# Moving the transposes of q, k and the attention output from TensorE to crossbar DMA, with a reordered start

## The chip, the cores and the metric

The kernel runs on one core of a Trainium2 chip. The metric is device time of one execution in microseconds (us). Each number quoted as a result is the median of several executions; most executions of one kernel agree within about 0.3%. All runs quoted here are in the fast state. Ratios are the mean time of one kernel's fast runs over the mean of the other kernel's fast runs of the same rounds, so they are not quite the ratio of the medians quoted beside them. In the profiles PE is TensorE, DVE is VectorE, ACT is ScalarE, POOL is GpSimd and SP is SyncE; SBUF and PSUM are the two on-chip memories that hold the kernel's tiles, with the matmul results in PSUM.

## The reference, cut to what matters

```python
# q, k, v: (8 batches, 8 heads, 576 positions, 64), float32
scores = matmul(q, k^T) / 8 + bias[bucket(|i - j|)]      # T5 relative bias, 32 buckets
x = softmax(scores) @ v                                   # (8, 8, 576, 64)
x = x.transpose(0, 2, 1, 3).reshape(4608, 512)
h = x @ w_in                                              # 512 -> 2048
out = max(0.01 * h, h) @ w_out                            # 2048 -> 512, float32
```

## The kernel before

Two heads form a pair, and there are 32 pairs, four to a batch. For each pair the kernel computes scores transposed (keys on partitions), takes the exponential on ScalarE, multiplies the diagonal band by the exponentiated bias on VectorE, and multiplies with v on TensorE (`av`). The feed-forward part is cut into 288 *pieces* of four 512-wide matmuls, and up to eight pieces are put into each pair as filler for TensorE. A tile of 512 tokens can start only when all the attention output that it reads is finished; whatever was not placed runs in a tail after the last pair.

Three operands have to be turned: q and k of the pair (12 blocks of 96x128) and the attention output (5 blocks of 128x128, the last half empty). All turns go through TensorE into PSUM, and are copied out:

```python
def transpose_q(n):
    qs = prs.pop((n, "q"))
    ps = ps_m_pool.tile([P, 8 * P], BF16, name="ps_tq", tag="m")
    for c in range(NC):                                   # NC = 6
        nc.tensor.transpose(ps[:, c * RQ : (c + 1) * RQ], in_=qs[0:RQ, c, :], identity=ident[0:RQ, 0:RQ])
    ...  # copied to qt by VectorE (ScalarE in pairs 1 to 3)
# transpose_k: the same, into kt
def x_transposes(n):
    ...
    for ic in range(NJ + 1):                              # 5 blocks
        nc.tensor.transpose(ps[:, ic * P : (ic + 1) * P], in_=opair[:, ic, :], identity=ident)
    nc.vector.tensor_copy(out=xT[p][:, b * S : (b + 1) * S], in_=ps[:, 0:S])
```

The order of work inside pair n, shortened (`moe(k)` places up to k pieces, alternating between the first and the second layer):

```python
    pair_rows(n + 1)                     # gathers the pair's q and k rows, VectorE
    scores 0, 1;  moe(1);  av(n - 1, 0);  transpose_q(n + 1);  moe(1)
    scores 2, 3;  moe(1);  av(n - 1, 1);  transpose_k(n + 1);  moe(1)
    scores 4, 5;  moe(1);  x_transposes(n - 1);  finished(n - 1);  moe(1);  moe(2)
moe_rest()                               # after the last pair
```

`finished` releases the token tiles that a batch completes. At the start, the bias rows come from DRAM in the order `hk` for heads 0 and 1, `hk` for heads 2 to 7 (576 KB), `hk4` for the last 64 keys.

The softmax here doesn't subtract the row's maximum and nothing guards it: scores larger than these inputs give would overflow.

Of the kernel before, what the change touches and what calls it, by code (L numbers as in the profile page):

```python
# [11 lines left out]
BF16 = mybir.dt.bfloat16  # L12
# [25 lines left out]
def kernel(  # L38
# [10 lines left out]
    nc = tc.nc  # L49

    B, H, S, D = q.shape
    NB, HH = bias_table.shape
    DM, DF = moe_w_in.shape
    NT = B * S
# [15 lines left out]
    per = ctx.enter_context(tc.tile_pool(name="per", bufs=1))  # L70
    qt_pool = ctx.enter_context(tc.tile_pool(name="qt", bufs=2))
    pr_pool = ctx.enter_context(tc.tile_pool(name="pr", bufs=4))
    op_pool = ctx.enter_context(tc.tile_pool(name="op", bufs=2))
    rc_pool = ctx.enter_context(tc.tile_pool(name="rc", bufs=4))
    gt_pool = ctx.enter_context(tc.tile_pool(name="gt", bufs=2))
# [7 lines left out]
    nc.vector.memset(warm, 0.0)  # L83
    nc.scalar.activation(warm, warm, AF.Exp)

    xT = [per.tile([P, NT], BF16, name=f"xT{p}") for p in range(n_pairs)]
    w_in_sb = per.tile([P, n_cc, DF], BF16, name="w_in_sb")
    w_out_sb = per.tile([P, n_fc, DM], BF16, name="w_out_sb")
    hk = per.tile([P, H, 3 * P], BF16, name="hk")
# [16 lines left out]
    def load_qk(b, h0, h1):  # L106
        i = b % NBUF
        for src, dst in ((q, qn[i]), (k, kn[i])):
            nc.gpsimd.dma_start(
                out=dst[0:RQ, h0:h1, :, :].rearrange("r h c d -> r h (c d)"),  # L110
                in_=src[b, h0:h1, :, :].rearrange("h (r c) d -> r h (c d)", c=NC),
            )

    def load_v(b, h0, h1, by_head):
        i = b % NBUF
        p0, p1 = h0 // 2, h1 // 2
        if by_head:
            for h in range(h0, h1):
                nc.gpsimd.dma_start(
                    out=vn[i][:, :, h, 0:D],  # L120
                    in_=v[b, h, 0 : NJ * P, :].rearrange("(c s) d -> s c d", s=P),
                )
        else:
            for c in range(NJ):
                nc.gpsimd.dma_start(  # L125
                    out=vn[i][:, c, h0:h1, 0:D],
                    in_=v[b, h0:h1, c * P : (c + 1) * P, :].rearrange("h s d -> s h d"),
                )
        for e in range(2):
            nc.gpsimd.dma_start(  # L130
                out=v4[i][e * SL : (e + 1) * SL, p0:p1, e, 0:D],
                in_=v[b, h0 + e : h1 : 2, NJ * P : S, :].rearrange("h s d -> s h d"),
            )

    def clear(eng, i):
        eng.memset(v4[i], 0.0)
        for e in range(2):
            eng.memset(v4[i][e * SL : (e + 1) * SL, :, e, D : D + 1], 1.0)
        eng.memset(vn[i][:, :, :, D : D + 1], 1.0)
        eng.memset(kts_[i][:, S : S + P], 0.0)  # L140
        eng.memset(at_[i][:, ATW : ATW + SL], 1.0)
        eng.memset(at4_[i][:, S : S + SL], 1.0)

    junk = per.tile([P, 512], BF16, name="junk")
    nc.vector.memset(junk, 0.0)
    clear(nc.vector, 0)
    tabT = per.tile([H, NB], FP32, name="tabT")
    with nc.allow_non_contiguous_dma(reason="a table of 256 numbers"):
        nc.sync.dma_start(out=tabT, in_=bias_table.rearrange("u h -> h u"))
# [27 lines left out]
    )  # L177
    udr = nc.dram_tensor("u_row", [H, UW], BF16, kind="Internal")
    nc.sync.dma_start(out=udr.ap(), in_=ub)
    for h0, h1 in ((0, 2), (2, H)):  # L180
        nc.sync.dma_start(
            out=hk[:, h0:h1, :],
            in_=bass.AP(tensor=udr, offset=h0 * UW, ap=[[1, P], [UW, h1 - h0], [1, BW]]),
        )

    for e in range(2):
        nc.sync.dma_start(
            out=hk4[e * SL : (e + 1) * SL, :, :],
            in_=bass.AP(tensor=udr, offset=e * UW + SL + P, ap=[[1, SL], [2 * UW, n_pairs], [1, P + SL]]),
        )  # L190

    def mirrored(t, lo, hi):

# [4 lines left out]
        return bass.AP(tensor=v.tensor, offset=v.offset + hi - lo - 1, ap=ap)  # L198

    load_qk(0, 2, H)  # L200
    load_v(0, 0, 2, True)
    load_v(0, 2, H, False)
    clear(nc.gpsimd, 1)
    load_qk(1, 0, H)

    def load_w_in(half):
# [1 line left out]
        nc.gpsimd.dma_start(out=w_in_sb[:, :, o], in_=moe_w_in[:, o].rearrange("(c p) f -> p c f", p=P))  # L208

    def load_w_out(half):  # L210
        n = n_fc // 2
        nc.gpsimd.dma_start(
            out=w_out_sb[:, half * n : (half + 1) * n, :],
            in_=moe_w_out[half * n * P : (half + 1) * n * P, :].rearrange("(f p) e -> p f e", p=P),
        )


    items = [(b, p) for b in range(B) for p in range(n_pairs)]
    qts, kts, ops_ = {}, {}, {}

    prs = {}

    def pair_rows(n, which):
        src = {"q": qn, "k": kn}[which]
        b, p = items[n]
        t = pr_pool.tile([RQ, NC, 2 * D], BF16, name="pr")
        nc.vector.tensor_copy(out=t.rearrange("r c (e d) -> r c e d", e=2),
                              in_=src[b % NBUF][0:RQ, 2 * p : 2 * p + 2, :, :].rearrange("r e c d -> r c e d"))
        prs[n, which] = t

    def transpose_q(n):
        qs = prs.pop((n, "q"))
        ps = ps_m_pool.tile([P, 8 * P], BF16, name="ps_tq", tag="m")
        for c in range(NC):
            nc.tensor.transpose(ps[:, c * RQ : (c + 1) * RQ], in_=qs[0:RQ, c, :],  # L235
                                identity=ident[0:RQ, 0:RQ])
        qt = qt_pool.tile([P, S], BF16, name="qt")
        o, x = qt.rearrange("p (r c) -> p r c", c=NC), ps[:, 0:S].rearrange("p (c r) -> p r c", c=NC)
        if 0 < n < n_pairs:
            nc.scalar.copy(out=o, in_=x)  # L240
        else:
            nc.vector.tensor_copy(out=o, in_=x)  # L242
        qts[n] = qt

    def transpose_k(n):
        ks = prs.pop((n, "k"))
        ps = ps_m_pool.tile([P, 8 * P], BF16, name="ps_tk", tag="m")
        for c in range(NC):
            nc.tensor.transpose(ps[:, c * RQ : (c + 1) * RQ], in_=ks[0:RQ, c, :],  # L249
                                identity=ident[0:RQ, 0:RQ])  # L250
        kt = kts_[n % 2]
        nc.vector.tensor_copy(out=kt[:, 0:S].rearrange("p (r c) -> p r c", c=NC),  # L252
                              in_=ps[:, 0:S].rearrange("p (c r) -> p r c", c=NC))
        for e in range(2):
            r = slice(e * D, (e + 1) * D)
            nc.vector.tensor_copy(out=kt[r, S + e * SL : S + (e + 1) * SL], in_=kt[r, NJ * P : S])
        kts[n] = kt

    def qk_mm(n, u):

# [55 lines left out]
    def av(n, e):  # L316
# [7 lines left out]
        for ic in range(NJ + 1):  # L324
            for c in range(NJ):
# [7 lines left out]
        nc.vector.tensor_tensor(out=opair[:, :, e * D : (e + 1) * D], in0=ps[:, :, 0:D],  # L333
                                in1=rcp.to_broadcast([P, NJ + 1, D]), op=ALU.mult)

    def x_transposes(n):
        b, p = items[n]
        opair = ops_[n]
        ps = ps_m_pool.tile([P, 8 * P], BF16, name="ps_tx", tag="m")
        for ic in range(NJ + 1):  # L340
            nc.tensor.transpose(ps[:, ic * P : (ic + 1) * P], in_=opair[:, ic, :], identity=ident)  # L341
        nc.vector.tensor_copy(out=xT[p][:, b * S : (b + 1) * S], in_=ps[:, 0:S])
# [52 lines left out]
    def moe(n_pieces):  # L395
        nonlocal turn
        for _ in range(n_pieces):
            piece(("in", "out")[turn], False)
            turn ^= 1
# [5 lines left out]
    def finished(n):  # L405
        b, p = items[n]
        if p == n_pairs - 1:
            while made["ready"] < n_tt and (made["ready"] + 1) * TT <= (b + 1) * S:
                made["ready"] += 1


    pw = ps_o_pool.tile([P, 512], FP32, name="ps_w", tag="ps_o")
    for _ in range(14):
        nc.tensor.matmul(pw, lhsT=junk[:, 0:P], rhs=junk, start=True, stop=True)

    pair_rows(0, "q")
    pair_rows(0, "k")
    transpose_q(0)
    transpose_k(0)
    N = len(items)  # L420
    for n in range(N + 1):
        live = n < N
        if live:
            b, p = items[n]
            if n == 0:
                load_w_in(0)
                load_v(1, 0, H, False)
                load_w_in(1)
                load_w_out(0)
                load_w_out(1)  # L430
            elif p == 1 and 0 < b < B - 1:
                load_qk(b + 1, 0, H)
                load_v(b + 1, 0, H, False)
            if n + 1 < N:
                pair_rows(n + 1, "q")
                pair_rows(n + 1, "k")
            ps_a, ps_b = qk_mm(n, 0), qk_mm(n, 1)
            exp_band(n, 0, ps_a)
        moe(1)
        if live:  # L440
            exp_band(n, 1, ps_b)
        if n > 0:
            av(n - 1, 0)
        if n + 1 < N:
            transpose_q(n + 1)
        moe(1)
        if live:
            ps_a, ps_b = qk_mm(n, 2), qk_mm(n, 3)
            exp_band(n, 2, ps_a)
        moe(1)  # L450
        if live:
            exp_band(n, 3, ps_b)
        if n > 0:
            av(n - 1, 1)
        if n + 1 < N:
            transpose_k(n + 1)
        moe(1)
        if live:
            ps_a, ps_b = qk_mm(n, 4), qk_mm(n, 5)
            exp_band(n, 4, ps_a)  # L460
        moe(1)
        if n > 0:
            x_transposes(n - 1)
            finished(n - 1)
        moe(1)
        if live:
            exp_band(n, 5, ps_b)
        moe(2)
# [31 lines left out]
```

## Time and profile before

| | before |
|---|---|
| median time | 417.23 us (416.54 to 417.75, 3 runs) |
| span in the profile | 414.7 us |
| one pair in the steady part | 11.08 us |
| one pair without filler (pairs 2 to 4) | about 6 us |

The windows view of the kernel before gives, for a stretch of time, the busy time of each engine with the number of instructions, in the order PE, PE weight loads, VectorE, ScalarE, GpSimd, and then the granted TensorE clock as a share of full speed, the DMA share and GB/s. These rows are the starting phase, two moments of it, and the steady part:

```profile
0.00:27.00 27.00, 20.16 (x178) 10.50 (x179) 15.60 (x62) 14.43 (x19) 19.90 (x37) 0.75 1.24 172
16.00:18.00 2.00, 1.48 (x19) 1.05 (x18) 1.14 (x3) 0.94 (x2) 2.00 (x3) 0.50 1.69 193
18.00:20.00 2.00, 0.22 (x5) 0.23 (x6) 0.54 (x3) 0.00 (x0) 1.15 (x2) 0.50 1.42 195
110.00:330.00 220.00, 220.00 (x2316) 113.35 (x2314) 134.24 (x334) 147.37 (x199) 23.95 (x30) 1.00 0.35 52
```

The first busy number is PE. From 110 to 330 us TensorE is busy for all of the 220 us, while VectorE (134.24) and ScalarE (147.37) have slack. (The DMA share exceeds 1 in some rows, so it is used here only to compare.) At 18 to 20 us TensorE does almost nothing, and its clock is at half.

What a transpose costs has to be read from starts, not from the duration of one matmul, because matmuls overlap. The timeline of the kernel before, on TensorE (start, length, engine, line, what it does, how many merged), for the six q, six k and five output transposes, each followed by the next work, and the same matmul in two successive pairs:

```profile
226.27 0.42 PE L235 MATMUL ps_tq<-ident,pr 96*128 96x96 bf16 x6
226.53 1.03 PE L364 MATMUL pm_3608<-w_out_sb,gt 128*128 128x512 bf16 x4
...
229.66 0.42 PE L249 MATMUL ps_tk<-ident,pr 96*128 96x96 bf16 x6
229.92 1.03 PE L364 MATMUL pm_3608<-w_out_sb,gt 128*128 128x512 bf16 x4
...
231.10 0.39 PE L275 MATMUL ps_s<-qt,kt_107 128*128 128x512 bf16 x1
...
232.22 0.44 PE L341 MATMUL ps_tx<-ident,opair 128*128 128x128 bf16 x5
232.50 1.03 PE L364 MATMUL pm_3608<-w_out_sb,gt 128*128 128x512 bf16 x4
...
242.18 0.39 PE L275 MATMUL ps_s<-qt,kt_108 128*128 128x512 bf16 x1
```

The q transposes hold TensorE from 226.27 to 226.53 us, 0.26 us; k likewise 0.26 us; the output 0.28 us. That is 0.80 us of an 11.08 us pair. The Trainium skill's page "VectorE: DVE Perf Modes", section The three transpose paths, gives 390 ns for a 128x128 transpose on TensorE; here the trace shows a mean of 219 ns for one, and five of them take 0.28 us together because they are pipelined.

The waits view of the kernel before (who waited for whom: total us, times, longest) has one line that belongs to the start:

```profile
DVE at_0_111 L314 <- DMA hk_98<-u_row: 2.3, 1, 2.3
```

VectorE waits 2.3 us for `hk4` in pair 0, and TensorE waits behind it. This is the hole at 18 to 20 us.

### The profile page before, as it was taken

What the parts mean: (1) busy time and instruction counts of PE and PEld (TensorE: products, weight loads), DVE (VectorE), ACT (ScalarE), POOL (GpSimd) and SP (SyncE); (2) the same over time, 40 slices, a digit from 0 to 9 for tenths busy, and PEclk for the clock granted to TensorE, in tenths of its full rate; (3) what the DMA queues carried; (4) which work ended last, traced back from release to release, by engine and by line L of the source; (5) the groups of instructions that cost most, each with busy time, mean ns of one, the idle gap of its engine ahead of it and who ended that gap; (6) DMA issues with size and microseconds to landing.
All of it is one profiled execution on the core that took longest, in us unless ns stands there. A gap on an engine that the chain in (4) does not pass through costs nothing.

```text
span 414.7 us, 9081 instructions
## 1 busy us (share of the span) xinstructions
PE 397.0 (96%) x3886; PEld 204.0 (49%) x3886; DVE 222.7 (54%) x573; ACT 248.2 (60%) x342; POOL 59.8 (14%) x87
## 2 busy tenths in 40 slices
PE   7688899999999999999999999999999999999995
PEld 3355455554555555555445554555555454444442
DVE  5489776666666566655665566666556430101011
ACT  2688688766666766666666666667676633333310
POOL 8732410410040102210041004000000000000000
PEclk9589999999999999999999999999999999999999
DMA  8999993917063801872093509100000001010112
GB/s 116 204 197 196 206 163 54 60 32 135 27 42 44 141 26 34 78 115 52 27 82 61 107 28 81 30 19 9 25 27 27 28 27 51 25 53 25 51 51 77
DMA packets 60513, 29.37 MB, mean 71 GB/s; under 512 B 39472, under 2 KB 54840, under 8 KB 60472
## 3 DMA queue, kind: packets, MB, share of 16 engines
q0 software_dynamic: 53408, 18.35, 41.4%
q1 hardware_dynamic: 7064, 10.43, 7.2%
q8 instruction: 30, 0.49, 0.5%
q14 instruction: 11, 0.09, 0.1%
HBM read 37.68 MB, written 9.45 MB: 114 GB/s over the span
## 4 chain that ended last, share of the span: by engine, by line
PE 83%; DVE 7%; ACT 4%; DMA 3%; issue 1%; SPq 0%; DVEq 0%; ACTq 0%
PE ps_o L327 8%; PE ps_s L266 7%; PE ps_s L275 2%; DMA hk_98<-u_row 2%; PE ps_o L329 2%; PE ps_tx L341 2%; PE ps_tq L235 1%; ACT at_109 L286 1%; ACT at_110 L286 1%; PE ps_tk L249 1%; DVE at_109 L314 1%; PE ps_s L272 1%; DMA u_row<-ub 1%; DVE opair L333 1%; ACT gt L355 1%
## 5 line engine op out<-in xcount | busy, mean ns | idle before, releaser
L353 PEld LDWEIGHTS <-w_in_sb 128*128 128x128 bf16 x576 | 49.9, 98 | 72.6 <-issue 21.7
L364 PEld LDWEIGHTS <-gt 128*128 128x128 bf16 x576 | 52.5, 98 | 51.4 <-issue 0.4
L286 ACT ACTIVATE at_109<-ps_s 128x1024 bf16<-128x1024 f32 x64 | 64.5, 1023 | 20.5 <-PE ps_s L266 20.4
L286 ACT ACTIVATE at_110<-ps_s 128x1024 bf16<-128x1024 f32 x64 | 64.7, 1021 | 15.7 <-PE ps_s L266 15.7
L314 DVE TENSOR_TENSOR at_110<-at_110,hk 128x512 bf16<-128x512 bf16 (+1 forms) x64 | 32.2, 506 | 44.5 <-ACT at_110 L286 40.6
L314 DVE TENSOR_TENSOR at_109<-at_109,hk 128x512 bf16<-128x512 bf16 (+1 forms) x64 | 32.0, 506 | 38.6 <-ACT at_109 L286 36.4
L327 PEld LDWEIGHTS <-at_109 128*128 128x128 bf16 x640 | 28.5, 99 | 10.3 <-DVE opair L333 3.0
L333 DVE TENSOR_TENSOR opair<-ps_o,rcp 128x320 bf16<-128x320 f32 x64 | 31.5, 492 | 2.2
L327 PEld LDWEIGHTS <-at_110 128*128 128x128 bf16 x640 | 27.2, 98 | 9.6 <-DVE opair L333 3.0
L125 POOL DMA_DIRECT2D vn_104<-in_v_dram x16 | 14.1, 892 | 72.2 <-PE ps_o L329 71.2
L266 PE MATMUL ps_s<-qt,kt_107 64*128 64x512 bf16 x128 | 20.9, 388 | 2.8 <-DVE kt_107 L252 1.5
L125 POOL DMA_DIRECT2D vn_103<-in_v_dram x16 | 14.0, 887 | 61.7 <-PE ps_o L329 60.0
L242 DVE COPY qt<-ps_tq 128x576 bf16<-128x576 bf16 x29 | 21.7, 748 | 1.8 <-PE ps_tq L235 1.8
L266 PE MATMUL ps_s<-qt,kt_108 64*128 64x512 bf16 x128 | 20.9, 396 | 0.9 <-ACT at_110 L286 0.5
L332 DVE RECIPROCAL rcp<-ps_o 128x5 f32<-128x5 f32 x64 | 12.2, 191 | 11.6 <-PE ps_o L329 11.6
L327 PE MATMUL ps_o<-vn_103,at_109 128*128 128x65 bf16 x320 | 16.3, 200 | 1.1 <-DVE opair L333 0.7
L329 PEld LDWEIGHTS <-at_0_111 128*128 128x128 bf16 x160 | 15.9, 99 | 2.5 <-DVE at_0_111 L314 2.5
L327 PE MATMUL ps_o<-vn_103,at_110 128*128 128x65 bf16 x320 | 14.5, 194 | 1.7 <-DVE opair L333 1.7
L329 PE MATMUL ps_o<-v_0_105,at_0_111 128*128 128x65 bf16 x80 | 13.8, 200 | 2.2 <-DVE at_0_111 L314 2.2
L329 PEld LDWEIGHTS <-at_1_112 128*128 128x128 bf16 x160 | 15.6, 97 | 0.2 <-DVE at_1_112 L314 0.2
L341 PEld LDWEIGHTS <-opair 128*128 128x128 bf16 x160 | 11.3, 98 | 7.6 <-DVE opair L333 0.9
L288 ACT ACTIVATE at_110<-ps_s 128x512 bf16<-128x512 f32 x16 | 9.6, 598 | 9.1 <-PE ps_s L272 9.1
(873 smaller groups left out, 815.2 us busy)
## 6 DMA issues: line engine op xcount, KB each, us to landing
out_dram<-y SPq DMA_DIRECT2D x36, 256.0 KB, 2.0
qn_100<-in_q_dram POOLq DMA_DIRECT2D x4, 576.0 KB, 6.6
kn_102<-in_k_dram POOLq DMA_DIRECT2D x4, 576.0 KB, 9.6
w_in_sb<-in_moe_w_in_dram POOLq DMA_DIRECT2D x2, 1024.0 KB, 13.5
vn_104<-in_v_dram POOLq DMA_DIRECT2D x16, 128.0 KB, 4.8
w_out_sb<-in_moe_w_out_dram POOLq DMA_DIRECT2D x2, 1024.0 KB, 16.9
qn_99<-in_q_dram POOLq DMA_DIRECT2D x3, 576.0 KB, 7.0
kn_101<-in_k_dram POOLq DMA_DIRECT2D x3, 576.0 KB, 9.3
```

The costliest lines, as they stand in the source:

```text
L125: nc.gpsimd.dma_start(out=vn[i][:, c, h0:h1, 0:D], in_=v[b, h0:h1, c * P : (c + 1) * P, :].rearrange("h s d -> s h d"),)
L242: nc.vector.tensor_copy(out=o, in_=x)
L266: nc.tensor.matmul(ps[:, e, :], lhsT=kt[r, u * P : (u + 1) * P], rhs=qt[r, 0:512], start=True, stop=True)
L286: nc.scalar.activation(at[:, :, u, 0:512], ps, AF.Exp, scale=scale)
L314: nc.vector.tensor_tensor(out=o, in0=o, in1=m, op=ALU.mult)
L327: nc.tensor.matmul(ps[:, ic, :], lhsT=at[:, o : o + P], rhs=vn[i][:, c, 2 * p + e, :], start=(c == 0), stop=False)
L329: nc.tensor.matmul(ps[:, ic, :], lhsT=at4[:, ic * P : (ic + 1) * P], rhs=v4[i][:, p, e, :], start=False, stop=True)
L332: nc.vector.reciprocal(rcp, ps[:, :, D : D + 1])
L333: nc.vector.tensor_tensor(out=opair[:, :, e * D : (e + 1) * D], in0=ps[:, :, 0:D], in1=rcp.to_broadcast([P, NJ + 1, D]), op=ALU.mult)
L341: nc.tensor.transpose(ps[:, ic * P : (ic + 1) * P], in_=opair[:, ic, :], identity=ident)
L353: nc.tensor.matmul(pm, lhsT=w_in_sb[:, c, f * P : (f + 1) * P], rhs=xT[c][:, t0 : t0 + TT], start=(c == 0), stop=(c == n_cc - 1))
L364: nc.tensor.matmul(pm, lhsT=gt[:, f, ts * P : (ts + 1) * P], rhs=w_out_sb[:, f, :], start=(f == 0), stop=(f == n_fc - 1))
```

## The change: intent and diff

The intent is to take the transposes off TensorE. A DMA transpose through the crossbar turns the blocks while copying them from SBUF to SBUF. To keep out of the way of the first loads, q and k go by DMA only from pair 10 and the output from pair 6. The rest of the change prepares the start: bias rows for the last keys come before those of heads 2 to 7, a few memsets move from GpSimd to VectorE, w_out is loaded in batch 1, the loads of later batches are spread over the pairs, and "spin" matmuls on zeros keep TensorE busy in pair 0 (at the very start there were 14 of them before and are 15 now). The core of the diff:

```diff
+    load_hk(0, 2)
     for e in range(2): ... hk4 ...
+    load_hk(2, H)
...
+    AHEAD = 3
+    def by_dma(n):
+        return n >= 2 * n_pairs + 2
+    def turn_by_dma(n):
+        t = turned[n] = tu_pool.tile([P, 2 * NC, RQ], BF16, name="tu")
+        nc.sync.dma_start_transpose(out=t, in_=prs.pop(n).rearrange("r j c d -> r (j c d)"))
+    def turned_pair(n, j):
+        if by_dma(n):
+            return turned[n][:, j * NC : (j + 1) * NC, :].rearrange("p c r -> p r c")
+        ...  # six TensorE transposes as before
...
+    def x_by_dma(n):
+        return n_pairs + 2 <= n < N - 1
     def x_transposes(n):
+        if x_by_dma(n):
+            nc.sync.dma_start_transpose(
+                out=xT[p][:, b * S : b * S + w].rearrange("p (i t) -> p i t", t=P),
+                in_=opair.rearrange("p i d -> p (i d)"))
+            return
...
+            elif 0 < b < B - 1:          # loads spread over the pairs of a batch
+                if p < 2:
+                    load_qk(b + 1, 4 * p, 4 * p + 4)
+                if b == 1 and p > 0:
+                    load_w_out(p - 1)
+                if p > 0:
+                    load_v_part(b + 1, p - 1)
+            if n + AHEAD < N and by_dma(n + AHEAD):
+                pair_rows(n + AHEAD)
+                turn_by_dma(n + AHEAD)
...
+        if n > 1 and x_by_dma(n - 2):
+            finished(n - 2)              # in the middle of the pair, half a pair later than before
...
+    spin(15) before pair 0; in pair 0: spin(5), spin(3), spin(4)
```

The copies of q and k into their final order stay on VectorE; they now read the turned tile in SBUF in place of PSUM. All DMA transposes are issued from one queue. The Trainium skill's page "DMA: Bandwidth & Descriptors", section DMA Transpose (X-bar), says that two streams of transposes in flight at once can corrupt each other silently.

More of the change, by code (lines that the diff above doesn't have):

```diff
@@ L72 @@
     pr_pool = ctx.enter_context(tc.tile_pool(name="pr", bufs=4))
+    tu_pool = ctx.enter_context(tc.tile_pool(name="tu", bufs=4))
     op_pool = ctx.enter_context(tc.tile_pool(name="op", bufs=2))
@@ L84 @@
     nc.scalar.activation(warm, warm, AF.Exp)
-    xT = [per.tile([P, NT], BF16, name=f"xT{p}") for p in range(n_pairs)]
+    xT = [per.tile([P, NT + P - SL], BF16, name=f"xT{p}") for p in range(n_pairs)]
     w_in_sb = per.tile([P, n_cc, DF], BF16, name="w_in_sb")
@@ L112, in load_qk, with load_v_part @@
             )
+    def load_v_part(b, j):
+        i = b % NBUF
+        for c in ((0,), (1, 2), (3,))[j]:
+            nc.gpsimd.dma_start(
+                out=vn[i][:, c, :, 0:D],
+                in_=v[b, :, c * P : (c + 1) * P, :].rearrange("h s d -> s h d"),
+            )
+        if j == 2:
+            for e in range(2):
+                nc.gpsimd.dma_start(
+                    out=v4[i][e * SL : (e + 1) * SL, :, e, 0:D],
+                    in_=v[b, e::2, NJ * P : S, :].rearrange("h s d -> s h d"),
+                )
     def load_v(b, h0, h1, by_head):
@@ L133, in load_v, with clear_v @@
             )
-    def clear(eng, i):
+    def clear_v(eng, i):
         eng.memset(v4[i], 0.0)
@@ L139, in clear, with clear_edges @@
         eng.memset(vn[i][:, :, :, D : D + 1], 1.0)
+    def clear_edges(eng, i):
         eng.memset(kts_[i][:, S : S + P], 0.0)
@@ L145 @@
     nc.vector.memset(junk, 0.0)
-    clear(nc.vector, 0)
+    clear_v(nc.vector, 0)
+    clear_edges(nc.vector, 0)
     tabT = per.tile([H, NB], FP32, name="tabT")
@@ L179, with load_hk @@
     nc.sync.dma_start(out=udr.ap(), in_=ub)
-    for h0, h1 in ((0, 2), (2, H)):
+    def load_hk(h0, h1):
         nc.sync.dma_start(
@@ L200 @@
     load_qk(0, 2, H)
+    clear_edges(nc.vector, 1)
     load_v(0, 0, 2, True)
     load_v(0, 2, H, False)
-    clear(nc.gpsimd, 1)
+    clear_v(nc.gpsimd, 1)
     load_qk(1, 0, H)
@@ L210, in load_w_out @@
     def load_w_out(half):
+        if half > 1:
+            return
         n = n_fc // 2
@@ L219, with pair_rows @@
     qts, kts, ops_ = {}, {}, {}
-    prs = {}
-    def pair_rows(n, which):
-        src = {"q": qn, "k": kn}[which]
+    N = len(items)
+    AHEAD = 3
+    prs, turned = {}, {}
+    def pair_rows(n):
         b, p = items[n]
-        t = pr_pool.tile([RQ, NC, 2 * D], BF16, name="pr")
-        nc.vector.tensor_copy(out=t.rearrange("r c (e d) -> r c e d", e=2),
-                              in_=src[b % NBUF][0:RQ, 2 * p : 2 * p + 2, :, :].rearrange("r e c d -> r c e d"))
-        prs[n, which] = t
@@ L231, in transpose_q @@
-    def transpose_q(n):
-        qs = prs.pop((n, "q"))
-        ps = ps_m_pool.tile([P, 8 * P], BF16, name="ps_tq", tag="m")
-        for c in range(NC):
-            nc.tensor.transpose(ps[:, c * RQ : (c + 1) * RQ], in_=qs[0:RQ, c, :],
-                                identity=ident[0:RQ, 0:RQ])
-        qt = qt_pool.tile([P, S], BF16, name="qt")
-        o, x = qt.rearrange("p (r c) -> p r c", c=NC), ps[:, 0:S].rearrange("p (c r) -> p r c", c=NC)
-        if 0 < n < n_pairs:
-            nc.scalar.copy(out=o, in_=x)
-        else:
-            nc.vector.tensor_copy(out=o, in_=x)
-        qts[n] = qt
@@ L245, in transpose_k @@
-    def transpose_k(n):
-        ks = prs.pop((n, "k"))
-        ps = ps_m_pool.tile([P, 8 * P], BF16, name="ps_tk", tag="m")
-        for c in range(NC):
-            nc.tensor.transpose(ps[:, c * RQ : (c + 1) * RQ], in_=ks[0:RQ, c, :],
-                                identity=ident[0:RQ, 0:RQ])
-        kt = kts_[n % 2]
-        nc.vector.tensor_copy(out=kt[:, 0:S].rearrange("p (r c) -> p r c", c=NC),
-                              in_=ps[:, 0:S].rearrange("p (c r) -> p r c", c=NC))
+        t = prs[n] = pr_pool.tile([RQ, 2, NC, 2 * D], BF16, name="pr")
@@ new lines, in pair_rows @@
+        for j, src in enumerate((qn, kn)):
+            nc.vector.tensor_copy(out=t[:, j, :, :].rearrange("r c (e d) -> r c e d", e=2),
+                                  in_=src[b % NBUF][0:RQ, 2 * p : 2 * p + 2, :, :].rearrange("r e c d -> r c e d"))
+    def by_dma(n):
[3 more added lines that the diff above has]
+        nc.sync.dma_start_transpose(out=t, in_=prs.pop(n).rearrange("r j c d -> r (j c d)"))
@@ new lines, in turned_pair @@
+    def turned_pair(n, j):
+        if by_dma(n):
+            return turned[n][:, j * NC : (j + 1) * NC, :].rearrange("p c r -> p r c")
+        ps = ps_m_pool.tile([P, 8 * P], BF16, name="ps_t", tag="m")
+        for c in range(NC):
+            nc.tensor.transpose(ps[:, c * RQ : (c + 1) * RQ], in_=prs[n][0:RQ, j, c, :],
+                                identity=ident[0:RQ, 0:RQ])
+        return ps[:, 0:S].rearrange("p (c r) -> p r c", c=NC)
+    def transpose_q(n):
+        qt = qts[n] = qt_pool.tile([P, S], BF16, name="qt")
+        copy = nc.scalar.copy if 0 < n < n_pairs else nc.vector.tensor_copy
+        copy(out=qt.rearrange("p (r c) -> p r c", c=NC), in_=turned_pair(n, 0))
@@ L254, in transpose_k @@
+    def transpose_k(n):
+        kt = kts[n] = kts_[n % 2]
+        nc.vector.tensor_copy(out=kt[:, 0:S].rearrange("p (r c) -> p r c", c=NC), in_=turned_pair(n, 1))
         for e in range(2):
@@ L256, in transpose_k @@
             nc.vector.tensor_copy(out=kt[r, S + e * SL : S + (e + 1) * SL], in_=kt[r, NJ * P : S])
-        kts[n] = kt
     def qk_mm(n, u):
@@ L338, in x_transposes @@
         opair = ops_[n]
+        w = (NJ + 1) * P
+        if x_by_dma(n):
+            nc.sync.dma_start_transpose(
+                out=xT[p][:, b * S : b * S + w].rearrange("p (i t) -> p i t", t=P),
+                in_=opair.rearrange("p i d -> p (i d)"),
+            )
+            return
         ps = ps_m_pool.tile([P, 8 * P], BF16, name="ps_tx", tag="m")
@@ L412, with spin @@
     pw = ps_o_pool.tile([P, 512], FP32, name="ps_w", tag="ps_o")
-    for _ in range(14):
-        nc.tensor.matmul(pw, lhsT=junk[:, 0:P], rhs=junk, start=True, stop=True)
-    pair_rows(0, "q")
-    pair_rows(0, "k")
+    def spin(k):
+        for _ in range(k):
+            nc.tensor.matmul(pw, lhsT=junk[:, 0:P], rhs=junk, start=True, stop=True)
+    spin(15)
+    pair_rows(0)
     transpose_q(0)
     transpose_k(0)
-    N = len(items)
+    spin(5)
     for n in range(N + 1):
@@ L428 @@
                 load_w_in(1)
-                load_w_out(0)
-                load_w_out(1)
-            elif p == 1 and 0 < b < B - 1:
-                load_qk(b + 1, 0, H)
-                load_v(b + 1, 0, H, False)
-            if n + 1 < N:
-                pair_rows(n + 1, "q")
-                pair_rows(n + 1, "k")
+            elif 0 < b < B - 1:
[5 more added lines that the diff above has]
+                    load_v_part(b + 1, p - 1)
+            if n + 1 < N and not by_dma(n + 1):
+                pair_rows(n + 1)
+            if n + AHEAD < N and by_dma(n + AHEAD):
+                pair_rows(n + AHEAD)
+                turn_by_dma(n + AHEAD)
             ps_a, ps_b = qk_mm(n, 0), qk_mm(n, 1)
@@ L445 @@
             transpose_q(n + 1)
+        if n == 0:
+            spin(3)
         moe(1)
@@ L456 @@
             transpose_k(n + 1)
+        if n == 0:
+            spin(4)
         moe(1)
@@ L463 @@
             x_transposes(n - 1)
-            finished(n - 1)
+            if not x_by_dma(n - 1):
+                finished(n - 1)
         moe(1)
```

## The prediction

> **What bounds the kernel now.** TensorE. The windows view shows PE busy for all of 110 to 330 us (220.00 of 220.00) and on to the last matmul; VectorE is 61% and ScalarE 67% busy there. In steady state one head pair takes about 11.05 us (mean spacing of the 576-wide exponentials, 199.6 to 332.2 us over 12 pairs). Before that, in the timeline, PE waits for ScalarE in pairs 5 to 8 (8.48 us a pair), and the first 27 us hold only 20 us of PE work, at half clock from 10 to 24 us (windows view, PEclk 0.50).
>
> **What is removed.** In the timeline at 226 us, six q transposes hold PE for 0.26 us start to start, six k transposes 0.26 us, five output transposes 0.28 us. The change takes away q and k for 22 pairs (11.4 us) and the output for 25 pairs (7.0 us): 18.4 us, nearly all in the PE-bound stretch. The trace of before holds a check: in pair 31, which has no q and k to transpose, the pair takes 10.56 us. VectorE loses 25 copies of 457 ns, off the critical path.
>
> **What is added.** Crossbar transposes from the sync queue: 96x1536 bf16 (295 KB) and 128x640 (164 KB) per pair. DMA is busy only 35% from 110 to 330 us. The Trainium skill, "DMA: Bandwidth & Descriptors", Latency and other measured facts, gives 261 GB/s for a DMA transpose; an estimate from it is 1.1 and 0.6 us plus about 2 us to land. "VectorE: DVE Perf Modes", The three transpose paths, gives 1309 ns for one 128x128 block by DMA; were the 17 blocks serial at that, a pair would need 22 us and DMA would be the new limit. No run here shows either. I take 3 to 8 us per transpose, hidden, as q and k have over two pairs (about 20 us) and the output about 10 us before use.
>
> **Feed-forward pieces.** Output tiles are released half a pair later. Counting pieces by the program, pairs 8 and 9 get 3 and 4 instead of 5 and 8, so six pieces (0.86 us each) move to the tail, and about one pair runs without filler. Pairs 2 to 4, without filler, take about 5.9 us for 3.9 us of PE work, so some 2.3 us of PE idle comes back.
>
> **Start.** VectorE waits 2.3 us for the edge bias table (waits view, DMA hk_98), PE 2.1 us behind it. The reordered loads and memsets, and spins that hold the clock, should give about 3 us. Moving w_out helps little: its waits are not on the chain.
>
> **Sum.** 417.2 - 18.4 - 3.0 + 2.3 + 1 (small stalls) = 399 us; range 393 to 408. Faster by over 2%: 0.86; within 2%: 0.10; slower: 0.04.
>
> **What would show each step.** Pair spacing about 10.25 us from pair 11 on, PE still without gaps; no wait of PE or VectorE on the transposed tiles; transposes landing in under 8 us; end of pair 1 about 3 us earlier with PEclk near 1 from 10 us; a PE gap of 2 to 3 us around pairs 8 to 9.
>
> **What would make it wrong.** Crossbar transposes slower than about 45 GB/s or slow to issue on the sync queue, so that PE waits on xT or on the q and k tiles; loads of q, k and v slowed by them, so that VectorE stalls on pair copies; the clock not held at the start.

## The result, and the profile after

The changed kernel takes 399.56 us (399.17 to 400.11, 4 runs) against 417.39 us in the same rounds; the ratio is 0.9577, 95% interval 0.9558 to 0.9596. Run again later beside other kernels it took 399.48 us, ratio 0.9587. The predicted time was 399.0 us.

The timeline of the changed kernel on TensorE, over the same work (start, length, engine, line, operation, count): the second half of `av`, the piece that now follows it directly, and the same score matmul in two successive pairs:

```profile
225.57 0.19 PE L355 MATMUL ps_o<-v_1_109,at_0_114 128*128 128x65 bf16 x1
225.59 1.03 PE L400 MATMUL pm_3475<-w_out_sb,gt 128*128 128x512 bf16 x4
226.56 0.29 PE L298 MATMUL ps_s<-qt,kt_111 64*128 64x64 bf16 x8
226.78 0.39 PE L301 MATMUL ps_s<-qt,kt_111 128*128 128x512 bf16 x1
...
234.47 0.38 PE L389 MATMUL pm_3711<-xT_95,w_in_sb 128*128 128x512 bf16 x1 [0.16 <-issue]
...
237.07 0.39 PE L301 MATMUL ps_s<-qt,kt_110 128*128 128x512 bf16 x1
```

From 226.78 to 237.07 us is 10.29 us: the pair is 0.79 us shorter, which is the 0.80 us of the transposes. It is so in every pair from 10 to 31 (10.28 to 10.31 us).

The windows view of the changed kernel, columns as above:

```profile
0.00:27.00 27.00, 20.78 (x190) 10.87 (x192) 16.39 (x66) 14.79 (x19) 19.24 (x34) 0.87 1.25 171
20.00:21.00 1.00, 0.05 (x2) 0.06 (x3) 0.97 (x4) 0.33 (x1) 0.87 (x2) 0.50 1.31 201
60.00:90.00 30.00, 26.44 (x319) 14.37 (x322) 20.86 (x58) 23.73 (x33) 8.08 (x11) 1.00 1.10 128
110.00:330.00 220.00, 215.94 (x2051) 106.65 (x2091) 125.54 (x314) 150.98 (x207) 27.12 (x36) 1.00 0.69 91
```

TensorE seems to have lost 4 us of its 220, but the line at 234.47 us above shows why: its group of four matmuls is listed with three, the one on xT_94 being absent from the trace, and the "issue" gap of 0.16 us stands in its place (there are 2051 matmul records and 2091 weight loads in that stretch). So TensorE is still the bound, with less to do. The DMA share doubled from 0.35 to 0.69.

The DMA issues of the changed kernel in the page (count, then median us from issue to landing), and the range of landing times of the q and k tile from the tile's view:

```profile
tu<-pr SPq DMA_TRANSPOSE x22, 3.4
xT_96<-opair SPq DMA_TRANSPOSE x7, 2.6
xT_97<-opair SPq DMA_TRANSPOSE x6, 7.1
xT_94<-opair SPq DMA_TRANSPOSE x6, 8.8
xT_95<-opair SPq DMA_TRANSPOSE x6, 2.7
```

```profile
DMA to landing us min/median/max: 3.3/3.4/13.5
```

A transpose of 295 KB lands 3.3 us after issue at best, as in pairs 26 to 28, the last that issue one, and 3.4 us in the median. The outputs of the last pair of a batch (xT_97) and of the first (xT_94) take 7 to 9 us: they fall in the stretches in which the next batch's q, k and v are loaded. The longest took 13.5 us (issued in pair 13, the second of its batch). A q and k transpose is issued at the start of pair n and its tile is first read in pair n + 2, 18.5 us later for the first tile (63.0 to 81.5 us) and 25.3 us later for the last (271.3 to 296.6 us), which covers even that; the tile's view lists no engine that waited for it.

At the start, the waits view of the changed kernel and its TensorE timeline show what came in place of the 2.3 us wait:

```profile
DVE at_113 L340 <- DMA hk<-u_row: 1.5, 1, 1.5
```

```profile
20.95 0.40 PE L353 MATMUL ps_o<-vn_106,at_112 128*128 128x65 bf16 x4 [2.60 <-DVE opair L359]
```

`hk4` now comes in time, but the rows of heads 2 to 7, which pair 1 needs, come last. In VectorE's timeline the band product of pair 1 waits 1.55 us for them and starts at 19.36 us; the normalization of the output of pair 0 comes only after it, at 20.40 us, and TensorE waits 2.60 us for that. The hole moved from pair 0 to pair 1; the clock, held at full speed up to 19 us, then falls to half (row 20 to 21 us above).

### The profile page after: what moved, and what is told of

Same layout as the page of the kernel before. It is cut to its first block, busy times and chain, and to the rows that moved or that the text cites. A ratio compares the mean times of both kernels' runs of the same rounds, so it can differ in the third digit from the quotient of the medians.

```text
span 398.3 us, 8365 instructions
## 1 busy us (share of the span) xinstructions
PE 374.6 (94%) x3449; PEld 187.3 (47%) x3510; DVE 210.7 (53%) x551; ACT 248.2 (62%) x342; POOL 66.3 (17%) x96
## 3 DMA queue, kind: packets, MB, share of 16 engines
q1 hardware_dynamic: 49912, 21.02, 28.3%
## 4 chain that ended last, share of the span: by engine, by line
PE 71%; DVE 15%; ACT 5%; DMA 4%; issue 4%; SPq 0%; DVEq 0%; ACTq 0%
PE ps_o L353 8%; PE ps_s L292 7%; DVE y L405 3%; DVE opair L359 3%; DMA hk<-u_row 2%; DVE at_113 L340 2%; PE ps_o L355 2%; ACT at_113 L312 2%; ACT at_112 L312 2%; DVE at_112 L340 2%; DVE kt_110 L280 1%; PE ps_s L301 1%; DVE kt_111 L280 1%; DMA u_row<-ub 1%; DVE rcp L358 1%
## 5 line engine op out<-in xcount | busy, mean ns | idle before, releaser
L118 POOL DMA_DIRECT2D vn_107<-in_v_dram x12 | 10.6, 900 | 82.4 <-PE ps_o L355 82.4
L118 POOL DMA_DIRECT2D vn_106<-in_v_dram x12 | 10.6, 902 | 68.5 <-PE ps_o L355 63.4
L353 PE MATMUL ps_o<-vn_106,at_112 128*128 128x65 bf16 x320 | 15.7, 197 | 4.8 <-DVE opair L359 4.3
L353 PE MATMUL ps_o<-vn_106,at_113 128*128 128x65 bf16 x320 | 15.2, 197 | 1.5 <-DVE opair L359 1.4
L353 PE MATMUL ps_o<-vn_107,at_112 128*128 128x65 bf16 x320 | 14.3, 194 | 0.1
L353 PE MATMUL ps_o<-vn_107,at_113 128*128 128x65 bf16 x320 | 14.3, 194 | 0.0
L276 DVE COPY qt<-tu 128x576 bf16<-128x576 bf16 x22 | 14.3, 648 | 0.0
```

Source lines behind the costliest of these rows:

```text
L118: nc.gpsimd.dma_start(out=vn[i][:, c, :, 0:D], in_=v[b, :, c * P : (c + 1) * P, :].rearrange("h s d -> s h d"),)
L276: copy(out=qt.rearrange("p (r c) -> p r c", c=NC), in_=turned_pair(n, 0))
L353: nc.tensor.matmul(ps[:, ic, :], lhsT=at[:, o : o + P], rhs=vn[i][:, c, 2 * p + e, :], start=(c == 0), stop=False)
```

## The experiments

All outputs are right. Where a run is set against the changed kernel, this is done through its ratio to the kernel before in the same rounds; the changed kernel's ratio is 0.9577 (interval 0.9558 to 0.9596) and 0.9587 (0.9566 to 0.9608) on the chip of the last three rows. The runs from last_on_pe to best ran on a chip on which the changed kernel itself was not run, so against it they can be set only through these ratios; among themselves they share their rounds.

| run | median us | ratio to before | 95% interval | steady pair, us |
|---|---|---|---|---|
| changed kernel | 399.56 | 0.9577 | 0.9558 to 0.9596 | 10.29 |
| no_dma_transposes | 415.52 | 0.9968 | 0.9949 to 0.9987 | 11.08 |
| qk_only | 403.60 | 0.9687 | 0.9653 to 0.9721 | 10.57 |
| x_only | 411.29 | 0.9872 | 0.9851 to 0.9893 | 10.80 |
| dummy_pe | 410.99 | 0.9859 | 0.9832 to 0.9886 | 10.80 |
| last_on_pe | 398.50 | 0.9566 | 0.9550 to 0.9583 | 10.29 / 10.58 |
| split_bias | 398.09 | 0.9552 | 0.9538 to 0.9566 | 10.29 |
| no_spin | 399.84 | 0.9592 | 0.9576 to 0.9608 | 10.29 |
| best | 396.70 | 0.9519 | 0.9503 to 0.9535 | 10.29 / 10.58 |
| ahead1 | 434.35 | 1.0414 | 1.0379 to 1.0449 | 10.3 to 19.5 |
| early_qk | 407.45 | 0.9771 | 0.9744 to 0.9799 | 10.29 |
| w_out_early | 400.74 | 0.9610 | 0.9589 to 0.9632 | 10.29 |

The steady pair is the distance between the same score matmul of successive pairs in the TensorE timeline.

### Which part carries the gain: no_dma_transposes, qk_only, x_only

The theory is that TensorE time taken out of a TensorE-bound stretch is the gain. The rival is that the start and the spread loads carry a good part.

```diff
 def by_dma(n):
-    return n >= 2 * n_pairs + 2
+    return False          # no_dma_transposes and x_only
 def x_by_dma(n):
-    return n_pairs + 2 <= n < N - 1
+    return False          # no_dma_transposes and qk_only
```

> The changed kernel with every transpose back on TensorE; spins, moved memsets, reordered bias loads and spread loads stay. My theory (the gain is TensorE time removed from a TensorE-bound stretch; the start gave only about 0.5 us): 416.9 us, between 416 and 418, pair spacing 11.08 us again. Rival (the spread loads and the start carry a good part of the gain): 405 to 413 us.

> Only q and k by DMA, outputs back on TensorE. Theory: 25 x 0.28 us come back, but tiles are released as before, so the 2.3 us lost around pairs 8 and 9 do not occur: 399.6 + 7.0 - 2.3 = 404.3 us, pair spacing 10.57 us, pair 9 about 10 us long. Rival (late release costs nothing): 406.6 us.

> Only outputs by DMA, q and k back on TensorE. Theory: 22 x 0.52 us come back: 411.0 us, pair spacing 10.80 us. Rival (VectorE copies out of PSUM matter as well, 749 ns against 648 ns): more than 412 us.

Without DMA transposes the time is 415.52 us, ratio 0.9968: all the rest of the change together gains 1.3 us (0.32% of 416.8 us), 0.5 to 2.1 us by the interval. This is outside the 405 to 413 us of the rival, and a little below the theory's 416 us. With q and k alone it is 403.60 us (theory 404.3; single times from 402.46 to 405.02), with the output alone 411.29 us (theory 411.0). The steady pairs are 11.08, 10.57, 10.80 and 10.29 us: 0.51 for q and k, 0.28 for the output, 0.79 for both. The parts simply add, which is what a single bound with two independent loads on it does.

### Is it TensorE time, or PSUM and VectorE: dummy_pe

The DMA path also removes PSUM tiles, and copies out of PSUM cost VectorE more than those from SBUF. This run leaves the DMA transposes in place, and puts equally many idle transposes back on TensorE, into a PSUM tile that no engine reads:

```diff
+        if by_dma(n):                    # in transpose_q and in transpose_k
+            ps = ps_m_pool.tile([P, 8 * P], BF16, name="ps_d", tag="m")
+            for c in range(NC):
+                nc.tensor.transpose(ps[:, c * RQ : (c + 1) * RQ], in_=ident[0:RQ, :],
+                                    identity=ident[0:RQ, 0:RQ])
```

> The changed kernel, with twelve transposes of the identity per pair put on TensorE for pairs 10 to 31, into a PSUM tile that nobody reads; q and k still come by DMA, so the result is right. Theory (what counts is TensorE time alone): 399.6 + 11.4 = 411.0 us, the same as x_only. Rival (the gain is the relief of PSUM buffers' readers or of VectorE): near 400 us.

It took 410.99 us, the same as x_only (411.29), with the same steady pair of about 10.8 us. The score matmul of two successive pairs of this run in the TensorE timeline:

```profile
232.69 0.39 PE L311 MATMUL ps_s<-qt,kt 128*128 128x512 bf16 x1
243.50 0.39 PE L311 MATMUL ps_s<-qt,kt 128*128 128x512 bf16 x1
```

So occupying TensorE alone gives back the whole of what q and k by DMA had gained. VectorE's lighter load is visible in the groups view (648 ns for a q copy out of the turned tile, 749 ns out of PSUM) but worth nothing here, since VectorE was not the bound. (The dummies also take a PSUM tile each, which no run separates from the time on TensorE; the 0.51 us by which the pair grows is the 0.52 us that the twelve transposes hold TensorE.)

### The late release of token tiles: last_on_pe

A DMA transpose cannot be used at once, so the change calls `finished` half a pair later. Counting pieces by the program: pairs 8 and 9 hold 3 and 4 pieces instead of 5 and 8, and six pieces move to the tail. In this run the last pair of each batch, which releases a tile, goes through TensorE:

```diff
 def x_by_dma(n):
-    return n_pairs + 2 <= n < N - 1
+    return n_pairs + 2 <= n < N - 1 and n % n_pairs != n_pairs - 1
```

> The changed kernel, but the last pair of each batch (7, 11, 15, 19, 23, 27) has its output transposed on TensorE, so that its tile is released as in the kernel before. Theory (late release leaves about one pair without filler and costs 2.3 us): pair 9 is about 10 us long again instead of 6.66, six transposes of 0.28 us come back, net 399.0 us, 0.6 us faster than the changed kernel. Rival (the late release costs nothing): 401.3 us.

The score matmul of pairs 8, 9 and 10 in the TensorE timelines, first of the changed kernel and then of this run:

```profile
76.05 0.38 PE L301 MATMUL ps_s<-qt,kt_110 128*128 128x512 bf16 x1 [0.31 <-ACT at_112 L312]
82.71 0.39 PE L301 MATMUL ps_s<-qt,kt_111 128*128 128x512 bf16 x1
92.99 0.39 PE L301 MATMUL ps_s<-qt,kt_110 128*128 128x512 bf16 x1
```

```profile
74.90 0.38 PE L301 MATMUL ps_s<-qt,kt 128*128 128x512 bf16 x1 [0.31 <-ACT at L312]
84.87 0.39 PE L301 MATMUL ps_s<-qt,kt 128*128 128x512 bf16 x1
95.15 0.39 PE L301 MATMUL ps_s<-qt,kt 128*128 128x512 bf16 x1
```

The distance from pair 8 to pair 9 is 6.66 us in the changed kernel and 9.97 us here: the filler is back, 3.3 us of it. The tail, from the score matmul of pair 31 to the end of the span, is 89.2 us in the changed kernel (309.1 to 398.3) and 83.9 us here (312.7 to 396.6), 5.3 us shorter. So the late release costs 5.3 - 3.3 = 2.0 us. Against this stand later pairs of 10.58 instead of 10.29 us, five of them, 1.45 us. What remains, about 0.5 us, is within the interval: the whole run is 398.50 us and its ratio interval overlaps that of the changed kernel. The mechanism is shown by the profile; that this version is faster is not shown by the times of this run alone. The profiles can leave the start out: from the score matmul of pair 2 to the end of the span it is 368.0 us here and 367.9 us in best, which has the same edit, against 368.6 to 368.7 us in both profiles of the changed kernel, in split_bias and in no_spin. That is 0.7 us for the edit.

### Why the start gained little: split_bias, no_spin, w_out_early

Theory: the wait for the bias rows of heads 2 and 3 took over from the wait for `hk4`. Rivals: loads of q, k, v, or the clock.

```diff
-    load_hk(2, H)
+    load_hk(2, 4)         # split_bias
+    load_hk(4, H)
```

> The changed kernel, with the 576 KB bias load for heads 2 to 7 split so that heads 2 and 3, which pair 1 needs, come first (192 KB), the other four after. Theory (the start gained little because VectorE now waits for these rows, 1.55 us, with TensorE idle 2.6 us behind it and the clock halved after that): 1 to 2.5 us faster than the changed kernel, 397.1 to 398.6 us. Rival (the start is held by the loads of q, k, v or by ScalarE): no difference, 399.6 us.

398.09 us, ratio 0.9552 against 0.9577 and 0.9587: 1.0 to 1.5 us faster by the ratios, at the lower end of what was expected, but the interval overlaps or touches both of the changed kernel's, so this run alone does not show it. The clean comparison is best (below) against last_on_pe: they differ by this edit alone and ran in the same rounds, with ratios of 0.9519 (0.9503 to 0.9535) and 0.9566 (0.9550 to 0.9583), which is 2.0 us. The windows view of split_bias, columns as above, and then that of the changed kernel for the same five microseconds:

```profile
15.00:20.00 5.00, 4.30 (x62) 2.98 (x63) 4.30 (x12) 3.21 (x5) 4.57 (x6) 0.66 1.44 222
20.00:25.00 5.00, 3.96 (x63) 2.38 (x59) 4.73 (x15) 4.68 (x7) 2.36 (x4) 1.00 1.29 207
```

```profile
15.00:20.00 5.00, 2.77 (x37) 1.52 (x36) 3.40 (x9) 3.98 (x5) 4.34 (x7) 0.97 1.45 219
20.00:25.00 5.00, 4.05 (x50) 2.95 (x50) 3.67 (x11) 1.56 (x3) 3.01 (x4) 0.50 1.28 207
```

TensorE is busy for 4.30 instead of 2.77 us between 15 and 20 us, and ScalarE for 4.68 instead of 1.56 us between 20 and 25 us. The distance from pair 0 to pair 1 is a poor measure here: it is 7.24 us, against 9.54 and 9.94 us in the two profiles of the changed kernel, but 7.06 us in x_only, which has the same start as these and only came late to pair 0. The position of pair 2's score matmul is safer, in the TensorE timelines first of the changed kernel and then of split_bias:

```profile
29.66 0.38 PE L301 MATMUL ps_s<-qt,kt_110 128*128 128x512 bf16 x1
```

```profile
26.58 0.39 PE L302 MATMUL ps_s<-qt,kt 128*128 128x512 bf16 x1
```

In best it is at 27.16 us. The eight profiles whose start is that of the changed kernel have it between 27.93 and 29.91 us, the kernel before at 29.82 us. So a single profile of the start varies by 2 us, but both with the split load come before all of the others. What the runs do not separate is the wait itself from the clock, which from 20 to 25 us was 1.00 in split_bias and 0.50 in the changed kernel.

```diff
-    spin(5); spin(3); spin(4)     # in pair 0
+    spin(0); spin(0); spin(0)     # no_spin
```

> The changed kernel without the 12 spin matmuls inside pair 0 (the 15 at the very start stay). Theory: clock at half from about 10 us on, as before; as this stage waits for loads and ScalarE, 0 to 1 us slower than the changed kernel. Rival (the held clock is what the start gained): 1.5 to 3 us slower.

399.84 us, ratio 0.9592, its interval overlapping both of the changed kernel's: the spins inside pair 0 bring nothing that these runs can tell (pair 2's score matmul is at 29.95 us, against 29.66 and 29.91 us). They do hold the clock: the windows view gives 0.75 from 10 to 15 us and 0.50 from 15 to 20 us without them, 1.00 and 0.97 with them; from 20 to 25 us both have 0.50. The Trainium skill's page "TensorE: Matmul & The Clock Gate", Part 1, says that TensorE's clock goes to half after at least one idle window of about 3.4 us; the trace agrees in direction, not in size: the changed kernel's clock falls between 19 and 20 us (mean 0.84 in that microsecond), inside a stretch without matmuls that lasts only 2.6 us, from 18.3 to 20.95 us. That the held clock brought nothing fits the 2.60 us for which TensorE had no work, behind the wait for bias rows.

```diff
 if n == 0: load_w_in(0); load_v(1, 0, H, False); load_w_in(1)
+           load_w_out(0); load_w_out(1)            # w_out_early
-if b == 1 and p > 0: load_w_out(p - 1)
```

> The changed kernel with both halves of w_out loaded in pair 0 again, as in the kernel before. Theory (this part of the change is not on the chain): within 1 us of the changed kernel, 399 to 400.5 us. Rival (w_out delays the loads of the first 60 us): 2 us or more slower.

400.74 us, ratio 0.9610 against 0.9587 on the same chip, with overlapping intervals: a difference of 1 us is neither shown nor excluded. The rival's 2 us or more is not seen.

### How much lead, and how early: ahead1, early_qk

```diff
-    AHEAD = 3
+    AHEAD = 1             # ahead1
```

> The changed kernel with the q and k transposes started one pair before use in place of three. They land 3.3 us after issue where no loads run and up to 13.5 us after where they do, and q is copied about 3 us after the issue. Theory (the lead of three pairs hides this and is needed): VectorE waits on the transposed tile, most in the pairs that share the DMA engines with loads; 5 to 40 us slower, 405 to 440 us. Rival (landing time has slack enough anyway): 399.6 us.

434.35 us, slower than the kernel before. The waits view of ahead1:

```profile
DVE qt L276 <- DMA tu<-pr: 38.4, 11, 8.1
...
PE pm L389 <- DVE y L405: 26.3, 8, 7.2
```

VectorE waits for the turned tile 11 times, 38.4 us in all, about the 35 us that the run lost. Its timeline shows its other work standing behind the q copy: after the longest wait the copy starts at 133.16 us, and the next band product, the normalization and the copy out of PSUM follow it one by one. TensorE in its turn waits 26.3 us in all for VectorE to empty a PSUM tile. The pairs reached at 146.7, 197.7 and 248.5 us took 19.1 to 19.5 us each, four pairs apart, in step with the loads of the next batch. A lead of two pairs was not run.

```diff
 def by_dma(n):
-    return n >= 2 * n_pairs + 2
+    return n >= n_pairs   # early_qk
```

> The changed kernel with q and k by DMA from pair 4 on in place of pair 10. Theory: pairs 4 to 9 are not bound by TensorE (8.48 us for about 7.4 us of its work), so at most 1 us can be gained, while pair copies need batch 1 three pairs earlier, when its loads have not landed, so VectorE waits: 402 to 408 us. Rival (removed TensorE work pays everywhere): 399.6 - 6 x 0.52 = 396.5 us.

407.45 us, within the theory's range and 8 us slower than the changed kernel. The waits view of early_qk:

```profile
DVE pr L253 <- DMA qn<-in_q_dram: 5.9, 2, 4.4
DVE pr L253 <- DMA kn<-in_k_dram: 4.6, 2, 2.6
```

With a lead of three pairs, pair 4 asks for batch 1 in pair 1, before its rows have landed: VectorE waits 4.4 us for q and 2.6 us for k (22.86 and 25.82 us in its timeline). The other two of the four waits, 1.5 and 2.0 us, are over by 12.2 us and concern batch 0; the changed kernel waits 2.3 us there too. From pair 0 to pair 1 it is 15.16 us in place of 9.5 to 9.9 in the changed kernel, and from pair 4 to pair 5 it is 11.28 us in place of 8.8. Nothing comes back in pairs 5 to 8, which stay at about 8.48 us with or without their q and k transposes on TensorE.

### A version that is faster than both: best

```diff
-    load_hk(2, H)
+    load_hk(2, 4)
+    load_hk(4, H)
-    return n_pairs + 2 <= n < N - 1
+    return n_pairs + 2 <= n < N - 1 and n % n_pairs != n_pairs - 1
```

> Split bias load and last pair of each batch on TensorE together. Theory: the two add up, 1.6 to 3.1 us faster than the changed kernel, 396.5 to 398.0 us. Rival: neither matters, 399.6 to 401.3 us.

396.70 us (396.24 to 397.46), ratio 0.9519, interval 0.9503 to 0.9535, which lies wholly below both intervals of the changed kernel. It is 2.4 to 2.8 us faster than the changed kernel by the ratios. That the release on time has a share in this is supported by the profile of last_on_pe and by the step from split_bias (0.9552) to best (0.9519), whose intervals do not overlap, though single times of the two do (396.98 to 398.39 and 396.24 to 397.46 us).

## Why the prediction was right, point by point

- **The bound.** It said TensorE from 110 us on. Right: with the same number of TensorE transposes put back as dummies, the time comes back (dummy_pe).
- **What is removed, 18.4 us.** It was built from start-to-start distances (0.26, 0.26, 0.28 us) and checked on pair 31 of the trace of before. Predicted pair 10.25 us, measured 10.29 us. From no_dma_transposes to the changed kernel, 415.52 - 399.56 = 16.0 us, which is 18.4 less the 2.0 us of the late release within half a microsecond.
- **The DMA cost.** "3 to 8 us per transpose, hidden": landings were 2.6 to 8.8 us in the median, with single ones of 13.5 us, and no engine waited. The sign "under 8 us" was missed for the first pair of each batch (8.8 us in the median) and for single tiles, without harm, because the lead was longer. The sentence that 1309 ns per block in series would have meant 22 us a pair was a real alternative, and it did not occur.
- **The late release.** Predicted 2.3 us lost, measured 2.0 us; predicted six pieces in the tail, measured 5.3 us there, as six of 0.86 us make. The cause of the estimate, that a pair without filler takes about 6 us, also held: that pair took 6.66 us, with TensorE idle for 2.05 us of it (windows view).
- **The start, 3 us.** This term was mis-sized: with everything but the DMA transposes the change gains 1.3 us (0.5 to 2.1). The prediction took the wait for `hk4` out of the chain and did not ask what the reordering puts last, which is the rows for pair 1. The sign that it gave, the end of pair 1 about 3 us earlier, did not appear: pair 2's score matmul came at 29.66 us instead of 29.82. Sending the rows for pair 1 first gave another 2.0 us (best against last_on_pe).
- **Small stalls, 1 us.** There were none in the steady part. This error and the one at the start had opposite signs, so the sum, 399.0 us, was closer to 399.56 us than its terms deserve.
- **Spins and w_out.** "Moving w_out helps little" is in line with the runs. The hope that the held clock was part of the 3 us was not supported (no_spin).

## What to carry to other kernels

Where one engine is the bound without gaps, cost a removed instruction by the distance between starts and multiply: the parts added up here to a few hundredths of a microsecond per pair. A DMA transpose was cheap here with a lead that covers its slowest landing (13.5 us here beside loads, four times the 3.3 us at best) and cost 35 us with a lead of one pair, because the engine that waited for it held up the bound engine as well (38.4 us and 26.3 us of waits in ahead1). When a load is moved forward, look at what now comes last and who needs it next, and when a result comes later, count the work that can no longer start.

## What the Trainium skill lacked or had wrong

- "DMA: Bandwidth & Descriptors", Latency and other measured facts, gives 261 GB/s for a DMA transpose, measured on one kernel with a non-contiguous middle dimension. Here 295 KB landed in 3.3 us at best, 89 GB/s with the fixed time included. The hardware queue's share of 16 engines' time rose from 7.2% of 414.7 us to 28.3% of 398.3 us for 10.6 MB more (21.02 - 10.43 MB), which is 10.6 MB / 82.9 us = 128 GB/s while busy, contention included; this is rough, since such shares can exceed 1. The page has no figure for an SBUF to SBUF transpose of this size.
- "VectorE: DVE Perf Modes", The three transpose paths, gives 1309 ns for one 128x128 block by DMA. It does not say that the blocks of one transfer overlap: twelve 96x128 blocks landed in 3.3 us, about 280 ns a block.
- No page read gives what loads beside it do to the landing time of a DMA transpose: 3.3 us at best, up to 13.5 us in the stretches with loads.
- No page read gives, for trn2 by name and for a size like these, how long one transpose holds the issuing queue: the tile's view shows 1245 to 4154 ns (median 1909) on the sync queue for the q and k transposes.
